# Opening a fused attention and MLP kernel with blocks of 256 keys instead of two blocks of 128

## The chip, the cores and the metric

The kernel runs on one core of a Trainium2 chip. The metric is the device time of one execution in microseconds (us). Before the change three runs gave 542.96, 543.40 and 543.49 us, with a median of 543.4 us.

## The reference

Three layers follow each other on a batch of 2 sequences with 768 tokens and a model width of 512.

- **Attention.** 8 heads of 64. A query sees the first 8 keys of its sequence and the 96 keys up to itself. A linear bias by distance (ALiBi) is added per head, then softmax, then the product with the values.
- **Channel MLP.** `xn = (x - mean) / sqrt(var + 1e-6) * g_ln`, then `x + relu(xn @ w_ch1) @ w_ch2`, with a hidden width of 2048.
- **Token mix.** `theta = x @ w_theta`, `zr = x * cos(theta)`, `zi = x * sin(theta)`, `u = x + w_tok_r @ zr + w_tok_i @ zi` over the tokens, and at last `u + relu(u @ w_ch)`.

Everything is wanted at float32 accuracy. The weights of the MLP and the mix come as 64-bit floats; they are decoded on the chip, and each weight is split into a high and a low part, so that a product becomes three fast matmuls.

## The kernel before, in words

**Tiles.** The 1536 tokens are 12 blocks of 128 (batch 0 has blocks 0 to 5, batch 1 has 6 to 11). The first block of each sequence (0 and 6) has no older keys: its window is its own 128 keys. The other ten have a window of 256: 96 previous keys, 32 global ones, and their own 128. The text calls them 128-key and 256-key blocks. `CHUNKS` (line 28) pairs the blocks and so sets the order `SEQ` in which the attention takes them. Before, it is `[0, 6], [1, 2], [3, 4], [5, 7], [8, 9], [10, 11]`: both 128-key blocks first.

**One block's attention** (lines 181 to 301) goes through the engines in turn. `load_qk` and `load_v` issue its DMAs on SyncE's queue. `scores` does the q-k matmuls on TensorE, two pairs of heads into the PSUM tag "s" and two into "h". `soften` subtracts the maximum on VectorE (line 213, one instruction per head) and takes the exponential on ScalarE (line 220, one per head). `flip_probs` transposes the probabilities on TensorE; ScalarE copies the even pairs out of PSUM (line 261) and VectorE the odd ones (line 263), each tag with one buffer. `values` multiplies with v, `lift_x` copies the sum out (line 286), `finish_x` transposes it and divides by the softmax sum, `layer_norm` normalises, and `make_xt` transposes the result for the MLP.

**The order in time.** Two 128-key blocks run first, pair of heads by pair of heads, in `head_step` (lines 829 to 862). Then comes a loop of cycles (lines 898 to 951) in which TensorE's order is written out by hand, while a planner orders the instructions of the other engines. Cycle t does the scores of the t-th 256-key block, the values of the block before it, and two items of the MLP:

```python
items = [(c, f) for c in range(NCH) for f in GROUPS[0]]
for t in range((LEAD + len(items)) // 2 + 1):
    j = 2 * t - LEAD
```

An item is one chunk of 256 tokens by one of the first four slices of the hidden width: `up` (`mlp_h`, line 421) and `down` (`mlp_o`, line 446). With `LEAD = 2` the items begin in cycle 1, so cycle 0 is attention without MLP beside it. The remaining slices (lines 953 to 977) and the token mix (lines 993 to 1015) come behind the loop.

**Weights.** The MLP needs its first eight weight pieces while the loop runs. `split_w` makes one piece: two decoding instructions on ScalarE (lines 357 and 361), two on VectorE (362 and 363), a rounding on ScalarE (384) and a subtraction on GpSimd (385). `pieces(t)` sets how many have been made by the end of a cycle: two in the head, five by the end of cycle 0, eight by the end of cycle 1.

**Spins.** `spin` (line 75) issues matmuls of zeros whose result nobody reads. They stand in the head and in cycle 0 only: 28 in the head's code and 24 in cycle 0 (tile names spin and idle).

**Bias.** `make_bias` (line 141) makes the bias tables, first the 128-wide ones on VectorE and then the 256-wide ones on ScalarE (line 170). It needs `n_local`, which a small DMA brings (tile words, line 815).

Of the kernel before, what the change touches and what calls it, by code (L numbers as in the profile page):

```python
# [27 lines left out]
CHUNKS = [[0, 6], [1, 2], [3, 4], [5, 7], [8, 9], [10, 11]]  # L28
# [5 lines left out]
PAD = 24  # L34


@with_exitstack
def kernel(ctx, tc, q, kwin, v, n_pair, g_ln, wall, out):
# [10 lines left out]
    SEQ = [t for ts in CHUNKS for t in ts]  # L49
    NCH = len(CHUNKS)  # L50
# [33 lines left out]
    x2 = [x2all[:, t, :] for t in range(NTT)]  # L84
    nhalf = keep.tile([P, 1], F32, name="nhalf")
# [43 lines left out]
    def behind_exp(n):  # L129
        es = ExitStack()  # L130
        es.enter_context(tc.issue_after(maxima[n]))
        es.enter_context(tc.issue_after(exps[n]))
        return es
# [7 lines left out]
    def make_bias():  # L141

        n = WIN + P
        rel, key, a = (at.tile([P, n], F32, tag="xn", name=f"bias_{x}", bufs=3) for x in ("rel", "key", "a"))
        io = dict(allow_small_or_imprecise_dtypes=True)
        v_ = nc.vector
        own = rel[:, P:n].rearrange("p (t c) -> p t c", c=P)
        old, first = slice(0, WIN), slice(WIN, n)
        nc.gpsimd.iota(own, [[0, 2], [-1, P]], base=0, channel_multiplier=1, **io)
        nc.gpsimd.iota(key[:, first], [[1, P]], base=0, channel_multiplier=0, **io)  # L150
        nc.gpsimd.iota(rel[:, 0:PREV], [[-1, PREV]], base=PREV, channel_multiplier=1, **io)
        nc.gpsimd.iota(key[:, PREV:P], [[1, GLOB]], base=0, channel_multiplier=0, **io)
        v_.memset(rel[:, PREV:P], FAR)
        v_.memset(key[:, 0:PREV], FAR)
        v_.memset(key[:, P:WIN], FAR)
        v_.tensor_scalar(a[:, P:n], rel[:, P:n], 0.0, FAR, ALU.is_lt, ALU.mult)
        v_.tensor_tensor(rel[:, P:n], rel[:, P:n], a[:, P:n], ALU.max)
        yield
        load_n()
        for part in (first, old):  # L160
            r, k_, a_ = rel[:, part], key[:, part], a[:, part]
            with behind_maximum(3 if part is old else None):
                v_.tensor_scalar(a_, r, nl, NEG, ALU.is_ge, ALU.mult)
                v_.tensor_scalar(k_, k_, ng, NEG, ALU.is_ge, ALU.mult)
            v_.tensor_tensor(r, a_, r, ALU.subtract)
            v_.scalar_tensor_tensor(r, k_, nl, r, ALU.subtract, ALU.max)
            for h in range(H):
                slope = 2.0 ** (-8.0 * (h + 1) / H)
                if part is old:
                    nc.scalar.activation(bias[h][:, part], r, AF.Copy, scale=slope / SCALE)  # L170
                else:
                    v_.tensor_scalar(bias[h][:, part], r, slope / SCALE, None, ALU.mult)
            yield
# [50 lines left out]
    def scores(b, i, ps_, startup):  # L224
# [9 lines left out]
        s = [ps("h" if (ps_[0] % 2 if startup else ps_[0]) else "s", [P, n, nk], f"s{b}_{i}_{ps_[0]}_{j}") for j in range(2)]  # L234
# [5 lines left out]
        if startup:  # L240
            spin("o", f"spin{b}_{ps_[0]}", 2)
        if startup:
            soften_all(b, i, ps_, s)
# [7 lines left out]
    def flip_probs(b, i, p, startup):  # L251
        nb = 2 if i else 1
        e = e_t.pop((b, i, p))
        pt_tag = ("o" if startup else "m") if p % 2 else "pt"
# [35 lines left out]
    def finish_x(b, i, startup):  # L290
# [5 lines left out]
        xp = ps("o" if startup else "s", [P, H, D], f"xp{t}")  # L296
# [284 lines left out]
    def early_steps():  # L581
# [11 lines left out]
        for t in range(NZ):  # L593
# [16 lines left out]
    def tok_part(b, s, d, part):  # L610

        w, z = toks[b, s], z_t[b * NQ + s]
# [63 lines left out]
    def general():  # L676
# [102 lines left out]
        for b in range(B):  # L779
# [6 lines left out]
            for i in range(NQ):  # L786
                t = b * NQ + i
                ap = ps("o", [P, DM], f"g_a{t}")
                for s in range(NQ):
                    for n in range(2):  # L790
                        at_ = (n * 2 * SA if i * P < SA else n * SB) + i * P
                        wt = w[TOK + s * NT + at_ // DM][:, at_ % DM:at_ % DM + P]
# [21 lines left out]
    words = keep.tile([P, 2, 2], I32, name="words")  # L814
    nc.sync.dma_start(words.rearrange("p n w -> p (n w)"), n_pair.bitcast(I32).partition_broadcast(P))
# [3 lines left out]
    bias_steps = make_bias()  # L819
# [3 lines left out]
    HEAD = len(CHUNKS[0])  # L823
    ROWS = range(NPAIR)

    def behind(n):
        return divmod(n, NPAIR)

    def head_step(n):

        t, p = divmod(n, NPAIR)
        if t < HEAD:
            if p == 0:
                loads_to(t + 2)
            scores(*blocks[t], [p], True)
        for lag, fn in ((2, lambda b, i, p: flip_probs(b, i, p, True)), (3, values)):
            if 0 <= n - lag < HEAD * NPAIR:
                t, p = divmod(n - lag, NPAIR)
                fn(*blocks[t], p)
                if lag == 3 and p == NPAIR - 1:  # L840
                    lift_x(*blocks[t])
                    finish_x(*blocks[t], True)

    spin("m", "spin", 12)
    for n in range(2):
        head_step(n)
    next(bias_steps)
    load_to(1)
    nc.sync.dma_start(gbc, g_ln.partition_broadcast(P))
    for n in range(2, 4):  # L850
        head_step(n)
    for n in range(4, HEAD * NPAIR):
        head_step(n)
        for d, m in enumerate((13, 15)):
            if n == m // 2:
                with behind_exp(m):
                    split_w(0, (d,))
        if n == 7:
            layer_norm(SEQ[0])
    with behind_maximum(7):  # L860
        test_n()

    NB = NTT - HEAD
    LEAD = 2
# [13 lines left out]
    def flips(t, ps_):  # L878
        if 0 <= t < NB:
            for p in ps_:  # L880
                flip_probs(*blocks[HEAD + t], p, False)

    made = []

    def pieces(t):
        n = (3,6)[t] if t < len((3,6)) else 2 * GROUP - 2
        if len(made) < n:
            with behind_exp(len(maxima) - 1):
                while len(made) < n:
                    m = len(made)  # L890
                    split_w(1 + m // 2, (m % 2,))
                    made.append(m)
        elif t >= 4:
            with behind_exp(len(maxima) - 1):
                decode_to(2 * GROUP + min(NW, t - 3))

    last1 = blocks[HEAD - 1]
    with tc.manual_schedule(engines={mybir.EngineType.PE}):
        for t in range((LEAD + len(items)) // 2 + 1):
            j = 2 * t - LEAD  # L900
            if t == 0:
                flip_probs(*last1, 2, True)
                values(*last1, 1)
                flip_probs(*last1, 3, True)
                spin("o", "idle0", 5)
            if t < NB:
                loads_to(HEAD + t + 2)
                sc = [scores(*blocks[HEAD + t], [0, 1], False)]
            if t == 0:
                values(*last1, 2)  # L910
                values(*last1, 3)
                lifted = lift_x(*last1)
            if t < NB:
                sc.append(scores(*blocks[HEAD + t], [2, 3], False))
                soften_all(*blocks[HEAD + t], [0, 1], sc[0])
            if 0 <= t - 1 < NB:
                for p in ROWS:
                    values(*blocks[HEAD + t - 1], p)
                lifted = lift_x(*blocks[HEAD + t - 1])
            if t < NB:  # L920
                with tc.issue_after(lifted):
                    soften_all(*blocks[HEAD + t], [2, 3], sc[1])
            if t == 0:
                spin("o", "idle3", 8)
                make_xt(SEQ[0])
                finish_x(*last1, True)
                layer_norm(SEQ[1])
                flips(0, (0, 1))
                spin("o", "idle1", 8)
                flips(0, (2, 3))  # L930
                make_xt(SEQ[1])
                spin("o", "idle2", 3)
                pieces(0)
                continue
            if t > NB:
                down(j - 1)
            up(j, "s")
            if t <= NB:
                finish_x(*blocks[HEAD + t - 1], False)
                layer_norm(SEQ[HEAD + t - 1])  # L940
            flips(t, (0, 1))
            if t <= NB:
                down(j - 1)
            up(j + 1, "h")
            flips(t, (2, 3))
            if t < NB:
                make_xt(SEQ[HEAD + t - 1])
            down(j)
            if t == NB:
                make_xt(SEQ[HEAD + t - 1])  # L950
            pieces(t)
# [31 lines left out]
    def more(t):  # L983
        if NZ <= t < NTT:
            for _ in theta(t):
# [8 lines left out]
    for n in range(NTT):  # L994
# [4 lines left out]
        for t in (NZ, NZ + 1) if n == 0 else (n + NZ + 1,):  # L999
            if t < NTT:  # L1000
                flip_x(t)
# [69 lines left out]
```

## Time and profile before

| | |
|---|---|
| median of three runs | 543.4 us |
| the profiled execution: its own time | 544.21 us |
| its span, first to last instruction | 542.1 us |
| TensorE matmul (PE) busy | 531.7 us, 98% |
| VectorE (DVE) busy | 361.7 us, 67% |
| ScalarE (ACT) busy | 284.5 us, 52% |
| GpSimd (POOL) busy | 20.3 us, 4% |
| DMA, mean over the span | 91 GB/s |

2.1 us of the profiled execution lie outside its span. A busy TensorE includes the spins, and matmuls overlap in the pipeline, so their pace is read from the distance between starts. PE, PEld, DVE, ACT and POOL are TensorE's matmuls, its weight loads, VectorE, ScalarE and GpSimd; SPq is SyncE's queue. L213 is line 213 of the kernel.

### The profile page before, as it was taken

What the parts mean: (1) busy time and instruction counts of PE and PEld (TensorE: products, weight loads), DVE (VectorE), ACT (ScalarE), POOL (GpSimd) and SP (SyncE); (2) the same over time, 40 slices, a digit from 0 to 9 for tenths busy, and PEclk for the clock granted to TensorE, in tenths of its full rate; (3) what the DMA queues carried; (4) which work ended last, traced back from release to release, by engine and by line L of the source; (5) the groups of instructions that cost most, each with busy time, mean ns of one, the idle gap of its engine ahead of it and who ended that gap; (6) DMA issues with size and microseconds to landing.
All of it is one profiled execution on the core that took longest, in us unless ns stands there. A gap on an engine that the chain in (4) does not pass through costs nothing.

```text
span 542.1 us, 8276 instructions
## 1 busy us (share of the span) xinstructions
PE 531.7 (98%) x3124; PEld 443.7 (82%) x3124; DVE 361.7 (67%) x791; ACT 284.5 (52%) x627; POOL 20.3 (4%) x31
## 2 busy tenths in 40 slices
PE   9998999999999999999999999999999999999996
PEld 4467888888888888888888887888888888888885
DVE  5789777877775455453558777986896689821532
ACT  4789766666734232333237556954885666720200
POOL 1223100100000000000000000000000000000000
PEclk9999999999999999999999999999999999999999
DMA  8946634422030232103224363220300000000122
GB/s 259 310 163 226 232 112 137 137 79 62 18 118 1 79 115 79 39 1 116 79 83 151 110 201 117 79 87 31 119 37 0 1 1 2 1 0 21 58 80 82
DMA packets 18543, 49.11 MB, mean 91 GB/s; under 512 B 2240, under 2 KB 4288, under 8 KB 18496
## 3 DMA queue, kind: packets, MB, share of 16 engines
q1 hardware_dynamic: 18496, 48.51, 26.4%
q8 instruction: 26, 0.43, 0.3%
q14 instruction: 21, 0.17, 0.1%
HBM read 45.35 MB, written 3.15 MB: 89 GB/s over the span
## 4 chain that ended last, share of the span: by engine, by line
PE 91%; ACT 4%; DVE 3%; issue 1%; ACTq 0%
PE op L446 24%; PE hp L421 24%; PE acc L621 18%; PE thm L544 6%; PE ch L667 6%; PE s L239 3%; PE xa L277 3%; PE pt L258 3%; ACT e L220 2%; PE spin L79 1%; PE xp L327 1%; PE xp L298 1%; PE xnp L327 1%; DVE w L363 1%; ACT dec L361 0%
## 5 line engine op out<-in xcount | busy, mean ns | idle before, releaser
L621 PE MATMUL acc<-tokh,z 128*128 128x256 f32 (+1 forms) x384 | 95.4, 336 | 0.0
L421 PE MATMUL hp<-xth,w1h 128*128 128x512 f32 (+1 forms) x240 | 84.3, 351 | 0.3 <-DVE nm L213 0.3
L421 PE MATMUL hp<-xtl,w1h 128*128 128x512 f32 (+1 forms) x240 | 83.2, 347 | 0.0
L421 PE MATMUL hp<-xth,w1l 128*128 128x512 f32 (+1 forms) x240 | 83.1, 346 | 0.0
L426 ACT ACTIVATE hh<-hp 128x512 fp32r<-128x512 f32 (+1 forms) x60 | 30.6, 510 | 97.7 <-PE hp L421 97.5
L446 PE MATMUL op<-w2h,hh 128*128 128x512 f32 x192 | 76.7, 400 | 0.0
L446 PE MATMUL op<-w2h,hl 128*128 128x512 f32 x192 | 75.2, 392 | 0.0
L446 PE MATMUL op<-w2l,hh 128*128 128x512 f32 x192 | 75.0, 390 | 0.0
L621 PEld LDWEIGHTS acc<-tokh,z 128*128 128x128 f32 x384 | 66.5, 190 | 8.0
L426 DVE SCALAR_TENSOR_TENSOR hl<-hp,hh 128x512 fp32r<-128x512 f32 (+1 forms) x60 | 34.8, 581 | 52.0 <-ACT hh L426 51.8
L621 PE MATMUL acc<-tokl,z 128*128 128x512 f32 (+1 forms) x192 | 64.5, 336 | 0.0
L220 ACT ACTIVATE e<-e,nm 128x256 f32<-128x256 f32 (+1 forms) x96 | 46.0, 483 | 23.6 <-DVE nm L213 23.4
L421 PEld LDWEIGHTS hp<-xth,w1h 128*128 128x128 f32 x240 | 45.3, 189 | 8.2 <-ACT e L220 1.2
L421 PEld LDWEIGHTS hp<-xtl,w1h 128*128 128x128 f32 x240 | 45.3, 189 | 6.2 <-DVE xtl L329 0.2
L421 PEld LDWEIGHTS hp<-xth,w1l 128*128 128x128 f32 x240 | 45.3, 189 | 5.6
L361 ACT ACTIVATE dec<-raw 128x512 int32<-128x512 uint32 x58 | 38.5, 664 | 9.6 <-DVE wt L363 5.9
L446 PEld LDWEIGHTS op<-w2h,hl 128*128 128x128 f32 x192 | 36.1, 188 | 8.3 <-DVE hl L426 0.8
L446 PEld LDWEIGHTS op<-w2l,hh 128*128 128x128 f32 x192 | 36.2, 188 | 6.8
L446 PEld LDWEIGHTS op<-w2h,hh 128*128 128x128 f32 x192 | 36.1, 188 | 6.5
L621 PEld LDWEIGHTS acc<-tokl,z 128*128 128x128 f32 x192 | 36.4, 190 | 4.0
L213 DVE CUSTOM_DVE_ANT_0 e<-s,bias 128x256 f32<-128x256 f32 (+1 forms) x96 | 32.8, 396 | 8.7 <-PE s L239 8.5
L520 ACT ACTIVATE tokh<-wt 128x512 fp32r<-128x512 f32 x36 | 22.1, 626 | 23.2 <-PE acc L621 18.1
(131 smaller groups left out, 918.7 us busy)
## 6 DMA issues: line engine op xcount, KB each, us to landing
raw<-in_wall SPq DMA_DIRECT2D x58, 512.0 KB, 3.5
k<-in_kwin SPq DMA_DIRECT2D x10, 512.0 KB, 4.9
q<-in_q SPq DMA_DIRECT2D x12, 256.0 KB, 3.8
vc<-in_v SPq DMA_DIRECT2D x12, 256.0 KB, 4.0
out<-o SPq DMA_DIRECT2D x8, 256.0 KB, 2.0
vw<-in_v SPq DMA_DIRECT2D x10, 192.0 KB, 4.2
out<-o SPq DMA_DIRECT2D x8, 128.0 KB, 2.1
vw<-in_v SPq DMA_DIRECT2D x10, 64.0 KB, 4.0
```

Of the source, the lines that this page charges most:

```text
L213: r = nc.vector.tensor_tensor_reduce(out=e[:, j, :], in0=s[j], in1=bias[h][:, b0:b0 + nk], scale=-SCALE, scalar=3.0e38, op0=ALU.add, op1=A ...
L220: r = nc.scalar.activation(e[:, j, :], e[:, j, :], AF.Exp, bias=nm[:, h:h + 1], scale=-1.0, accum_out=sm[:, h:h + 1])
L239: nc.tensor.matmul(s[j][:, a, :], qb[rows, p, :], kb[rows, p, k0:WIN], start=True, stop=True)
L258: nc.tensor.transpose(pt[:, j, c, :], e[:, j, c * P:(c + 1) * P], ident)
L361: nc.scalar.activation(t, r.bitcast(U32)[:, :, 0], AF.Copy, scale=2.0**-29 * (1 - 2.0**-15), bias=-0.4999)
L421: nc.tensor.matmul(hp, l, r[:, kk, :], start=(n == 0), stop=(n == 3 * KD - 1))
L426: r = nc.scalar.activation(hh, hp, AF.Relu), nc.vector.scalar_tensor_tensor(hl, hp, 0.0, hh.bitcast(F32), ALU.max, ALU.subtract)
L446: nc.tensor.matmul(op_t[c][j], l, r, start=(f == fs[0] and n == 0), stop=(f == fs[-1] and n == 2))
L520: nc.scalar.activation(hi, src, AF.Copy)
L544: nc.tensor.matmul(mp, l[:, kk, :], r[:, kk, :], start=(n == 0), stop=(n == 3 * KD - 1))
L621: mm = nc.tensor.matmul(o, l[:, dsl], r[:, sl], start=first and not (paired and d % 2), stop=end and not (paired and d % 2 == 0))
L667: nc.tensor.matmul(mp, l[:, kk, es], r, start=(kk == 0 and m == 0), stop=(kk == KD - 1 and m == 2))
```

## The change

The head is gone. The order of the blocks becomes `[1, 2], [3, 4], [5, 7], [8, 0], [9, 10], [11, 6]`, so that a 256-key block opens, and the 128-key blocks are the eighth and the last. All twelve go through the loop. `LEAD` becomes 6: the first MLP item stands in cycle 3, and cycles 0, 1 and 2 are attention alone. The scores of the second block are pulled into cycle 0 (`EARLY`). Five pieces of weights are due by the end of cycle 2 and eight by the end of cycle 3. The spins are 11 at the start and 4, 2 and 2 in cycle 0. The bias for 256 keys is made first, two heads on VectorE and six on ScalarE; the bias for 128 keys is made in cycle 5. The first block's q and k come in halves, its k on ScalarE's DMA queue. The test of `n` moves to cycle 8, and the decoding of the second group of weights starts one cycle later relative to the MLP items. The token mix takes its blocks in the order 1, 2, 3, 4, 5, 0 of each sequence, and the host rolls its weights to match. The core of the diff:

```diff
-CHUNKS = [[0, 6], [1, 2], [3, 4], [5, 7], [8, 9], [10, 11]]
+CHUNKS = [[1, 2], [3, 4], [5, 7], [8, 0], [9, 10], [11, 6]]
+DVE_BIAS = 2
+FIRST = 5
+EARLY = 1
+NPIECES = [(0, 1), (1, 3), (3, 5), (5, 8), (8, 8)]
+SPIN0 = 11
+SPINS = [(4, 2, 2)]
...
+    SORD = [*range(1, NQ), 0]
+    TORD = [b * NQ + s for b in range(B) for s in SORD]
...
+        for h in range(H):
+            slope = 2.0 ** (-8.0 * (h + 1) / H)
+            o = bias[h][:, 0:WIN] if old else bias[h][:, WIN:]
+            if h < DVE_BIAS:
+                v_.tensor_scalar(o, rel, slope / SCALE, None, ALU.mult)
+            else:
+                nc.scalar.activation(o, rel, AF.Copy, scale=slope / SCALE)
...
-        nc.sync.dma_start(qb, q[b, i])
-        nc.sync.dma_start(kb[:, :, k0:], kwin[b, i, :, :, k0:])
+        first = not qt
+        for a in ((0, 2), (2, 4)) if first else ((0, 4),):
+            a = slice(*a)
+            nc.sync.dma_start(qb[:, a], q[b, i, :, a])
+            (nc.scalar if first else nc.sync).dma_start(kb[:, a, k0:], kwin[b, i, :, a, k0:])
...
-    for n in range(4, HEAD * NPAIR):
-        head_step(n)
...
-    NB = NTT - HEAD
-    LEAD = 2
+    NB = NTT
+    LEAD = 6
...
     with tc.manual_schedule(engines={mybir.EngineType.PE}):
+        spin("m", "spin", SPIN0)
         for t in range((LEAD + len(items)) // 2 + 1):
             j = 2 * t - LEAD
+            sp = SPINS[t] if t < len(SPINS) else (0, 0, 0)
+            want = NPIECES[min(t, len(NPIECES) - 1)]
+            loads_to(t + 2)
+            score(t, LO)
+            score(t, HI)
+            soften_(t, LO)
             if 0 <= t - 1 < NB:
                 for p in ROWS:
-                    values(*blocks[HEAD + t - 1], p)
+                    values(*blocks[t - 1], p)
...
+            pieces(want[0])
...
+            if sp[0]:
+                spin("o", f"idle{t}", sp[0])
             up(j, "s")
...
+            flips(t, LO)
+            if t < EARLY:
+                score(t + 1, LO)
+                soften_(t + 1, LO)
...
+            if sp[1]:
+                spin("o", f"idle{t}b", sp[1])
             up(j + 1, "h")
+            flips(t, HI)
+            if t < EARLY:
+                score(t + 1, HI)
+            if 0 < t < NB:
+                make_xt(SEQ[t - 1])
+            if sp[2]:
+                spin("o", f"idle{t}c", sp[2])
             down(j)
...
+            if t == FIRST:
+                with behind_exp(len(maxima) - 1):
+                    for _ in make_bias(False):
+                        pass
```

## Rows read from the trace of the kernel before

**Rows 1.** Windows: length, then each engine's busy time (instructions), granted clock, DMA share, GB/s

```profile
7.00:22.95 15.95, 14.67 (x97) 7.64 (x93) 10.37 (x55) 13.38 (x50) 0.52 (x1) 1.00 1.01 355
22.95:34.81 11.86, 10.86 (x73) 6.49 (x72) 10.18 (x33) 9.06 (x26) 3.89 (x4) 1.00 0.56 189
34.81:47.94 13.13, 11.93 (x104) 10.03 (x103) 12.51 (x35) 11.51 (x32) 4.43 (x4) 1.00 0.65 220
47.94:61.40 13.46, 12.51 (x110) 10.87 (x109) 12.79 (x35) 10.31 (x28) 4.40 (x4) 1.00 0.63 217
61.40:135.11 73.71, 73.71 (x649) 65.08 (x648) 56.04 (x185) 47.63 (x142) 4.43 (x6) 1.00 0.33 110
538.00:542.00 4.00, 0.00 (x0) 0.00 (x0) 0.00 (x0) 0.00 (x0) 0.00 (x0) 0.71 0.13 45
```

**Rows 2.** Timeline of TensorE in cycle 3: start, us, line, output and inputs, count

```profile
61.40 2.00 PE L239 MATMUL s<-k,q 64*128 64x256 f32 x16
63.32 0.44 PE L277 MATMUL xa<-pts,vw 128*64 128x128 f32 x4
...
65.22 0.39 PE L421 MATMUL hp<-xth,w1h 128*128 128x256 f32 x1
...
66.75 0.60 PE L298 MATMUL xp<-ident,xs 128*128 128x128 f32 x4
67.19 1.04 PE L258 MATMUL pt<-ident,e 128*128 128x128 f32 x8
67.98 0.48 PE L446 MATMUL op<-w2h,hh 128*128 128x512 f32 x1
...
70.89 1.03 PE L258 MATMUL pt<-ident,e 128*128 128x128 f32 x8
71.76 0.60 PE L327 MATMUL xnp<-ident,xn 128*128 128x128 f32 x4
```

**Rows 3.** Timeline of TensorE in the head, a 128-key block

```profile
14.44 0.72 PE L239 MATMUL s<-k,q 64*128 64x128 f32 x8
15.08 0.44 PE L258 MATMUL pt<-ident,e 128*128 128x128 f32 x2
```

**Rows 4.** Timeline of the start: the spins, the wait for n, the bias of 256 keys

```profile
1.20 5.30 PE L79 MATMUL spin<-zero 128*128 128x512 bf16 x12 [1.20 <-DVE zero L121]
3.55 0.17 DVE L93 CAST low<-words 128x2 f32<-128x2 uint32 x1 [2.13 <-DMA words<-in_n]
11.66 2.55 ACT L170 ACTIVATE bias<-bias_rel 128x256 bf16<-128x256 f32 x8
```

**Rows 5.** Timeline of ScalarE in cycle 0, first and last of eight exponentials, a copy, a decode

```profile
26.76 0.50 ACT L220 ACTIVATE e<-e,nm 128x256 f32<-128x256 f32 x1
...
30.21 0.50 ACT L220 ACTIVATE e<-e,nm 128x256 f32<-128x256 f32 x1
...
31.18 0.59 ACT L261 ACTIVATE pts<-pt 128x512 f32<-128x512 f32 x1
31.66 0.69 ACT L357 ACTIVATE w<-raw 128x512 f32<-128x512 f32 x1
```

**Rows 6.** Timeline of VectorE in cycles 0 and 1: first and last of eight maxima, a copy, a decode

```profile
25.64 0.41 DVE L213 CUSTOM_DVE_ANT_0 e<-s,bias 128x256 f32<-128x256 f32 x1
...
28.04 0.41 DVE L213 CUSTOM_DVE_ANT_0 e<-s,bias 128x256 f32<-128x256 f32 x1
...
34.10 0.68 DVE L263 COPY pts<-pt 128x512 f32<-128x512 f32 x1
...
36.65 1.30 DVE L362 SCALAR_TENSOR_TENSOR dec<-w,dec 128x512 int32<-128x512 int32 x1 [0.25 <-ACT dec L361]
```

**Rows 7.** Timeline of TensorE at the end of cycle 0: spins, then the next cycle's scores

```profile
29.64 1.89 PE L79 MATMUL idle<-zero 128*128 128x512 bf16 x8
...
34.81 2.36 PE L239 MATMUL s<-k,q 64*128 64x256 f32 x16
```

**Rows 8.** SyncE's own waits up to 62 us: who waited for whom, us in total, times, longest

```profile
SPq L345 <- DVE w L363: 26.7, 8, 7.9
```

More of the change, by code (lines that the diff above doesn't have):

```diff
@@ L84 @@
     x2 = [x2all[:, t, :] for t in range(NTT)]
+    words = keep.tile([P, 2, 2], I32, name="words")
+    nc.sync.dma_start(words.rearrange("p n w -> p (n w)"), n_pair.bitcast(I32).partition_broadcast(P))
     nhalf = keep.tile([P, 1], F32, name="nhalf")
@@ L139, in behind_relu, with make_bias @@
         return es
-    def make_bias():
-        n = WIN + P
-        rel, key, a = (at.tile([P, n], F32, tag="xn", name=f"bias_{x}", bufs=3) for x in ("rel", "key", "a"))
+    def make_bias(old):
+        n = WIN if old else P
+        t = [at.tile([P, DM], F32, tag="xn", name=f"bias{old}_{x}", bufs=3) for x in ((0, 1, 2) if old else (0,))]
+        rel, key, a = (x[:, 0:n] for x in t) if old else (t[0][:, x * P:(x + 1) * P] for x in range(3))
+        own = slice(n - P, n)
         io = dict(allow_small_or_imprecise_dtypes=True)
@@ L146, in make_bias @@
         v_ = nc.vector
[L147 to L157, printed above, removed]
-        yield
[L159 to L173, printed above, removed]
+        if old:
+            nc.gpsimd.iota(rel[:, 0:PREV], [[-1, PREV]], base=PREV, channel_multiplier=1, **io)
+            nc.gpsimd.iota(key[:, PREV:P], [[1, GLOB]], base=0, channel_multiplier=0, **io)
+            v_.memset(rel[:, PREV:P], FAR)
+            v_.memset(key[:, 0:PREV], FAR)
+            v_.memset(key[:, P:WIN], FAR)
+        else:
+            nc.gpsimd.iota(key, [[1, P]], base=0, channel_multiplier=0, **io)
@@ new lines, in make_bias @@
+        nc.gpsimd.iota(rel[:, own], [[-1, P]], base=0, channel_multiplier=1, **io)
+        v_.tensor_scalar(a[:, own], rel[:, own], 0.0, FAR, ALU.is_lt, ALU.mult)
+        v_.tensor_tensor(rel[:, own], rel[:, own], a[:, own], ALU.max)
+        yield
+        if old:
+            load_n()
+        v_.tensor_scalar(a, rel, nl, NEG, ALU.is_ge, ALU.mult)
+        v_.tensor_scalar(key, key, ng, NEG, ALU.is_ge, ALU.mult)
+        v_.tensor_tensor(rel, a, rel, ALU.subtract)
+        v_.scalar_tensor_tensor(rel, key, nl, rel, ALU.subtract, ALU.max)
@@ L222, in soften, with scores @@
         e_t[b, i, p] = e
-    def scores(b, i, ps_, startup):
+    def scores(b, i, ps_):
         nk = WIN if i else P
@@ L233, in scores @@
         n = len(ps_)
-        s = [ps("h" if (ps_[0] % 2 if startup else ps_[0]) else "s", [P, n, nk], f"s{b}_{i}_{ps_[0]}_{j}") for j in range(2)]
+        s = [ps("h" if ps_[0] else "s", [P, n, nk], f"s{b}_{i}_{ps_[0]}_{j}") for j in range(2)]
         k0 = WIN - nk
@@ L295, in finish_x @@
         nc.vector.reciprocal(sm, sm)
-        xp = ps("o" if startup else "s", [P, H, D], f"xp{t}")
+        xp = ps("s", [P, H, D], f"xp{t}")
         for p in range(NPAIR):
@@ L591, in fill @@
                 next(ahead)
-        for t in range(NZ):
+        for t in TORD[:NZ]:
             while t not in ready:
@@ L822 @@
     loads_to(1)
-    HEAD = len(CHUNKS[0])
+    load_to(0)
     ROWS = range(NPAIR)
[L826 to L845, printed above, removed]
-        head_step(n)
[L847 to L851, printed above, removed]
-    for n in range(4, HEAD * NPAIR):
[L853 to L861, printed above, removed]
-    NB = NTT - HEAD
-    LEAD = 2
+    NB = NTT
+    LEAD = 6
     items = [(c, f) for c in range(NCH) for f in GROUPS[0]]
@@ L880, in flips, with pieces @@
             for p in ps_:
-                flip_probs(*blocks[HEAD + t], p, False)
+                flip_probs(*blocks[t], p)
     made = []
-    def pieces(t):
-        n = (3,6)[t] if t < len((3,6)) else 2 * GROUP - 2
+    def pieces(n):
         if len(made) < n:
@@ L890, in pieces, with score, soften_ @@
                     m = len(made)
-                    split_w(1 + m // 2, (m % 2,))
+                    split_w(m // 2, (m % 2,))
                     made.append(m)
[L893 to L897, printed above, removed]
+    sc = {}
+    def score(t, ps_):
+        if t < NB and (t, ps_) not in sc:
+            sc[t, ps_] = scores(*blocks[t], ps_)
+    def soften_(t, ps_):
+        if (t, ps_) in sc and sc[t, ps_]:
+            soften_all(*blocks[t], ps_, sc[t, ps_])
+            sc[t, ps_] = None
@@ L898 @@
+    LO, HI = (0, 1), (2, 3)
     with tc.manual_schedule(engines={mybir.EngineType.PE}):
+        spin("m", "spin", SPIN0)
         for t in range((LEAD + len(items)) // 2 + 1):
             j = 2 * t - LEAD
[L901 to L908, printed above, removed]
@@ L935 @@
+                lifted = lift_x(*blocks[t - 1])
+            with tc.issue_after(lifted) if t else ExitStack():
+                soften_(t, HI)
+            if t == 0:
+                nc.sync.dma_start(gbc, g_ln.partition_broadcast(P))
+            pieces(want[0])
             if t > NB:
                 down(j - 1)
+            if sp[0]:
+                spin("o", f"idle{t}", sp[0])
             up(j, "s")
-            if t <= NB:
-                finish_x(*blocks[HEAD + t - 1], False)
-                layer_norm(SEQ[HEAD + t - 1])
@@ L941 @@
-            flips(t, (0, 1))
+            if 0 < t <= NB:
+                finish_x(*blocks[t - 1])
+                layer_norm(SEQ[t - 1])
+            flips(t, LO)
+            if t < EARLY:
+                score(t + 1, LO)
+                soften_(t + 1, LO)
             if t <= NB:
                 down(j - 1)
+            if sp[1]:
+                spin("o", f"idle{t}b", sp[1])
             up(j + 1, "h")
-            flips(t, (2, 3))
-            if t < NB:
-                make_xt(SEQ[HEAD + t - 1])
+            flips(t, HI)
@@ L948 @@
+            if t < EARLY:
[4 more added lines that the diff above has]
+                spin("o", f"idle{t}c", sp[2])
             down(j)
             if t == NB:
-                make_xt(SEQ[HEAD + t - 1])
-            pieces(t)
+                make_xt(SEQ[t - 1])
+            pieces(want[1])
+            if want[1] == 2 * GROUP and t >= 7:
+                with behind_exp(len(maxima) - 1):
+                    decode_to(2 * GROUP + min(NW, t - 6))
@@ L953 @@
+            if t == FIRST:
+                with behind_exp(len(maxima) - 1):
+                    for _ in make_bias(False):
+                        pass
+            if t == 8:
+                with behind_exp(len(maxima) - 1):
+                    test_n()
     work = [(g, c, f) for g in range(1, len(GROUPS)) for c in range(len(WIDE)) for f in GROUPS[g]]
@@ L981, with more @@
     p2b_es, p2["b"] = stack(name="p2b", bufs=1)
-    def more(t):
-        if NZ <= t < NTT:
-            for _ in theta(t):
+    def more(n):
+        if NZ <= n < NTT:
+            for _ in theta(TORD[n]):
                 pass
```

48 lines of the change are left out of this document (12 added, 36 removed).

## The prediction

> **What bounds the kernel now.** I read the page first: TensorE is busy 98% of the span, so only TensorE time that is empty, or filled with spins, can be won. Then the busy time by windows, cut where each cycle's scores begin [rows 1]. From 61.40 to 135.11 us TensorE is busy 73.71 of 73.71 us: six cycles of 12.29 us bound by it, with VectorE and ScalarE at about three quarters and two thirds. Up to 61.40 us it is another kernel. In the two cycles before (13.13 and 13.46 us) VectorE works 12.51 and 12.79 us; in cycle 0 (11.86 us) it works 10.18 us, and there TensorE's busy time holds spins, such as the eight in 1.89 us [rows 7]. So all that the change can move lies before the point where TensorE gets its first closed cycle. I call that point S5 for the new kernel (the scores of cycle 5), which answers to 61.40 us (the scores of cycle 3) in the old one, as both have done four ups and three downs there.
>
> **What is left behind that point.** The old kernel has finished two 128-key blocks and is inside its third 256-key block; the new one is inside its fifth 256-key block and still owes both 128-key ones. All the rest is the same work, so the new kernel has less left, by two differences between a 256-key and a 128-key block. By starts in cycle 3 [rows 2], a 256-key block costs 63.32 - 61.40 = 1.92 us of scores, 65.22 - 63.32 = 1.90 us of values, and 0.79 + 0.87 = 1.66 us of flips (67.19 to 67.98, 70.89 to 71.76). A 128-key block has the same number of score instructions at half the columns: eight of its sixteen take 15.08 - 14.44 = 0.64 us [rows 3], so 1.28 us, not half. It has half the flips and half the values matmuls. The difference is 0.64 + 0.83 + 0.95 = 2.42 us, twice that 4.84 us. This holds if cycles 7, 8, 11 and 12 stay bound by TensorE. VectorE and ScalarE get less to do in them than in the six full cycles, where they have 56.0 and 47.6 of 73.7 us [rows 1], so I take all of it. If nothing of it came, the term would be 0.
>
> The sum is then: change = (S5 - 61.40) - 4.84.
>
> **The start.** Eleven spins instead of twelve at 5.30 / 12 = 0.44 us put the first scores at 1.20 + 4.86 = 6.06 us [rows 4]. They need half a q and half a k, less than the whole ones that the old kernel has by its first scores. The two k issues on ScalarE cost at most 1.3 us there (0.65 us for the old k issue) and lie before its first need. The bias cannot start before words lands (3.55 us); four 256-wide VectorE steps and the casting are about 1.7 us (estimate, from the 2.17 us that the old tables took from the same instant), so it is ready at 5.2 us. Six of the eight tables on ScalarE at 2.55 / 8 = 0.32 us [rows 4] end at 7.1 us, one instruction after VectorE has its first maxima.
>
> **Cycles 0 to 2.** The exponentials run at (30.21 - 26.76) / 7 = 0.49 us each, a copy or decode step at 31.66 - 31.18 = 0.48 to 0.56 us [rows 5], the maxima at (28.04 - 25.64) / 7 = 0.34 us [rows 6]. Along the chain:
> - Cycle 0: eight exponentials, 7.1 to 11.0. Copy, second flips, the pulled scores, four spins, values: 0.5 + 0.9 + 1.0 + 1.0 + 1.9, with about 0.2 for waits: 16.5 with the lift.
> - Cycle 1: the second block's first four exponentials are done in cycle 0; the last four with a maximum ahead: 2.4, to 18.9. Copy, flips, transposition for the MLP (0.4, estimate from the xp row): 2.2 with a wait, to 21.1.
> - Cycle 2: scores. In the old kernel they took 2.36 instead of 1.92 us behind such a transposition [rows 7], so 23.5. Values 25.4; lift, four exponentials and half a microsecond of weights on ScalarE, 28.7; copy, flips, transposition, 31.0.
>
> VectorE gives the other bound. From the pulled maxima (done at about 12.5 us) to that point it has: maxima of two blocks less the four already done, 12 x 0.34 = 4.1; five copies at 0.6, 3.0; two normalisations with the division, 2 x 2.25 = 4.5 (sum of five instructions by their spacing, estimate); two subtractions for the MLP, 1.2; three weight pieces at 1.2, and 0.6 for one of their steps that runs at 1.30 instead of about 0.68 us beside GpSimd [rows 6], 4.2. That is 17.0 us, and at the share that it reaches in the old cycles 1 and 2 (0.95) 17.9: 30.4. With the pulled maxima ending later, as they share VectorE with copies, I take S3 = 32.0 for the first scores of cycle 3. The old kernel stands at the same point, with five pieces due and two not finished, at 34.81 us. From there cycles 3 and 4 have the instructions of the old cycles 1 and 2, so S5 = 32.0 + 13.13 + 13.46 = 58.6.
>
> **Other edits.** The bias of 128 keys in cycle 5: three GpSimd instructions, some 1.5 us each on VectorE and ScalarE, beside 12.29 us of TensorE with over 2.9 us free on both: 0, and at most 1.5 us if it stood in the chain. Later decoding: the last pieces still come before the second group's first product; 0, at most 0.6 us a piece. The test of n: 0. The new mixing order leaves the count of matmuls; none of my rows shows a wait that it takes away or adds: 0, between -0.5 and +0.5.
>
> **Sum.** 58.6 - 61.4 - 4.84 = -7.6 us. The profiled execution took 544.2 us (542.1 of span and 2.1 around it): 536.6 for it. It lies 0.8 us above the median, so 535.8 us against 543.4. The ends: if VectorE never holds cycles 3 and 4, S5 is about 32.0 + 11 + 12.3 = 55.3, 532.5 us; if S3 is 3 us later, 538.8 us.
>
> **The clock.** The granted clock is 1.00 in every window up to 135 us, and 0.71 in the last four, where TensorE has no instruction left [rows 1]. The start shows what the low level costs: spins at 0.44 us there, and at 1.89 / 8 = 0.24 later [rows 4, 7]. The new cycles 1 and 2 have no spin and gaps of up to 1.5 us; the old kernel shows no such stretch without spins. [...]
>
> **Rivals.**
> [...]
> 2. The other side: VectorE and the chain through it keep the old pace. Each opening cycle takes 11.86 us, as the one old cycle without MLP does [rows 1]. S3 is 6.06 + 3 x 11.86 = 41.6, S5 68.2, +2.0: 545.4 us. It decides where S3 passes 34.81 + 4.84 = 39.65, that is above 11.2 us a cycle. Against it: that old cycle also finishes a 128-key block, normalises and transposes twice, and holds 19 spins.
> [...]
> 4. Transfers. The old start loads at 355 GB/s with the queue full to 22.95 us [rows 1]. Four whole blocks, g_ln and five pieces are 8.0 MB, 22.5 us of it, so from 2 us to about 25: enough, unless SyncE stops behind raw buffers, where it waited 26.7 us in all [rows 8]. Three microseconds lost: 538.8.
> 5. The cycles with 128 keys stay at 12.29 us, held by something else than TensorE: -2.8, 540.6 us.
>
> **How the numbers follow.** Forecast 0.61, with its own range from 532 to 540. Rival 1 once 0.10, twice 0.07; rival 2 0.07; rival 3 0.04; rival 4 0.06; rival 5 0.05. Runs of this kernel can tell about 0.2% (1.1 us) from no change. Faster: 0.61 + 0.10 + 0.06 + 0.05 = 0.82. Same: rival 1 twice, 0.07. Slower: rivals 2 and 3, 0.11. From 532 to 542 us holds the forecast, rival 1 once, and rivals 4 and 5: 0.82.
>
> **What would show it.** First scores at 6 us, S3 near 32 and S5 near 58.6, full cycles of 12.29 us after, and cycles 7 to 8 and 11 to 12 shorter by 2.4 us for each block. [...] The prediction is wrong if S3 comes after 36 us, or if something behind the loop moves by more than 0.5 us.

## The result, and the profile after

The changed kernel takes 537.6 us (median of five runs, 537.46 to 538.23) against 543.4 us (five runs, 542.96 to 543.92). The ratio is 0.9895, with a 95% interval of 0.9881 to 0.9910. The gain of 5.8 us lies inside the predicted range; the forecast was 7.6 us. The profiled execution took 537.60 us with a span of 535.8 us, 6.6 us less than the profiled one before, which lay 0.8 us above its median. The span is 6.3 us shorter.

The windows of the changed kernel, cut at its own cycles, have the columns of [rows 1]: length, busy time of PE, PEld, DVE, ACT and POOL, granted clock, DMA share, GB/s.

```profile
8.36:23.07 14.71, 11.64 (x95) 7.64 (x94) 11.19 (x41) 13.57 (x44) 1.84 (x2) 1.00 1.04 381
23.07:33.87 10.80, 7.79 (x73) 6.03 (x72) 10.11 (x31) 9.58 (x27) 3.04 (x3) 1.00 0.91 306
33.87:46.88 13.01, 12.14 (x104) 9.98 (x103) 11.51 (x34) 11.39 (x31) 3.55 (x4) 1.00 0.57 185
46.88:60.23 13.35, 12.51 (x110) 10.87 (x109) 12.79 (x35) 9.87 (x27) 4.79 (x6) 1.00 0.63 198
60.23:84.80 24.57, 24.57 (x217) 21.69 (x217) 18.48 (x67) 15.02 (x50) 1.10 (x2) 1.00 0.32 109
84.80:95.38 10.58, 10.58 (x102) 9.50 (x101) 7.17 (x30) 6.69 (x24) 0.55 (x1) 1.00 0.38 125
95.38:106.80 11.42, 11.42 (x93) 9.98 (x93) 10.65 (x42) 7.97 (x24) 0.92 (x1) 1.00 0.38 121
106.80:131.37 24.57, 24.57 (x217) 21.70 (x216) 19.29 (x63) 16.15 (x48) 1.47 (x2) 1.00 0.18 60
```

The reader is to see three stages. From the first exponential (8.36 us) to cycle 3 (33.87) ScalarE works 23.15 of 25.51 us, VectorE most of the second half, and TensorE has gaps. Cycles 3 and 4 (13.01 and 13.35 us) are those that were cycles 1 and 2 before, with nearly the same busy times [rows 1]. From 60.23 us on TensorE is closed. Full cycles still take 12.29 us; cycle 7, with the first 128-key block's scores and flips, takes 10.58, and cycle 8, with its values, 11.42.

The closed stretch that began at 61.40 us now begins at 60.23: 1.17 us. The first 128-key block gives 2 x 12.29 - 10.58 - 11.42 = 2.58 us. The second is read from TensorE's timelines: the scores of the last block and the first of its values, first in the changed kernel, then in the one before.

```profile
131.37 1.16 PE L255 MATMUL s<-k,q 64*128 64x128 f32 x16
141.95 1.09 PE L289 MATMUL xa<-pts,vc 128*64 128x128 f32 x16
...
135.11 2.00 PE L239 MATMUL s<-k,q 64*128 64x256 f32 x16
147.40 0.44 PE L277 MATMUL xa<-pts,vw 128*64 128x128 f32 x4
```

From one to the other it takes 10.58 us in place of 12.29, and the values themselves 1.02 us (the next product starts at 142.97) in place of 1.90 [rows 2]: 1.71 + 0.88 = 2.59 us. So the two 128-key blocks give 5.17 us where they stand, and the prediction had 4.84.

How much of it arrives is read where the token mix begins. The first token-mix product and the last, in one row for its line (duration, first and last start), after and before:

```profile
L633 PE MATMUL acc<-tokh,z x384: 277/336/478, 372.6 to 508.5; 128*128 128x512 f32 x96, 128*128 128x256 f32 x96
...
L621 PE MATMUL acc<-tokh,z x384: 277/336/476, 378.6 to 514.6; 128*128 128x512 f32 x96, 128*128 128x256 f32 x96
```

That is 6.0 us earlier at the first and 6.1 at the last, so the token mix keeps its length. 1.17 + 5.17 = 6.34 us were won up to the last values, so some 0.3 us are lost again between them and the token mix; what loses them is not shown.

The first instructions of the chain, from VectorE's and ScalarE's timelines of the changed kernel (the line numbers are its own):

```profile
3.75 0.17 DVE L103 CAST low<-words 128x2 f32<-128x2 uint32 x1 [2.33 <-DMA words<-in_n]
3.96 0.16 DVE L104 SCALAR_TENSOR_TENSOR nval<-words,low 128x2 f32<-128x2 int32 x1
4.23 0.35 DVE L176 TENSOR_SCALAR biasTrue<-biasTrue,nval 128x256 f32<-128x256 f32 x1
4.50 0.22 DVE L170 TENSOR_SCALAR biasTrue<-biasTrue 128x128 f32<-128x128 f32 x1
4.75 0.29 DVE L171 TENSOR_TENSOR biasTrue<-biasTrue,biasTrue 128x128 f32<-128x128 f32 x1
...
6.51 1.95 ACT L185 ACTIVATE bias<-biasTrue 128x256 bf16<-128x256 f32 x6 [3.35 <-DVE biasTrue L178]
8.36 0.49 ACT L236 ACTIVATE e<-e,nm 128x256 f32<-128x256 f32 x1
```

The bias was forecast for 5.2 us and ScalarE's tables for 7.1; they came at 6.5 and 8.4. L170 and L171 do not need n, and yet they stand behind the two instructions that wait for it. TensorE's waits in cycles 0 to 2 are on the copies and the lift of ScalarE, 5.2 us in all, but for 0.48 us on VectorE. Those of cycle 1:

```profile
18.22 0.66 PE L310 MATMUL xp<-ident,xs 128*128 128x128 f32 x4 [0.70 <-ACT xs L298]
18.71 1.04 PE L270 MATMUL pt<-ident,e 128*128 128x128 f32 x8
21.45 1.25 PE L270 MATMUL pt<-ident,e 128*128 128x128 f32 x8 [1.71 <-ACT pts L273]
22.54 0.60 PE L339 MATMUL xnp<-ident,xn 128*128 128x128 f32 x4
```

The granted clock stays at 1.00 in every window above, though from 17.5 to 23.1 us TensorE has transposes alone, with gaps of up to 1.71 us and no spin.

### The profile page after: what moved, and what is told of

Read it like the earlier page. It is cut to its first block, busy times and chain, and to the rows that moved or that the text cites. A ratio compares the mean times of both kernels' runs of the same rounds, so it can differ in the third digit from the quotient of the medians.

```text
span 535.8 us, 8220 instructions
## 1 busy us (share of the span) xinstructions
PE 522.2 (97%) x3091; PEld 439.7 (82%) x3091; DVE 361.0 (67%) x789; ACT 284.3 (53%) x631; POOL 19.6 (4%) x32
## 4 chain that ended last, share of the span: by engine, by line
PE 90%; ACT 5%; DVE 3%; issue 1%; DMA 1%; ACTq 0%; DVEq 0%
PE op L458 24%; PE hp L433 24%; PE acc L633 19%; PE thm L556 6%; PE ch L679 6%; PE pt L270 3%; PE xa L289 3%; PE s L255 2%; ACT e L236 2%; PE xp L339 1%; PE xp L310 1%; PE xnp L339 1%; DVE w L375 1%; DMA words<-in_n 1%; DVE e L229 1%
## 5 line engine op out<-in xcount | busy, mean ns | idle before, releaser
L446 DVE SCALAR_TENSOR_TENSOR x2all<-op,rsall,x2all 128x512 f32<-128x512 f32 x48 | 33.3, 741 | 2.1 <-PE op L458 2.1
```

The lines of the kernel that those rows point to most:

```text
L446: nc.vector.scalar_tensor_tensor(x2[t], o, rsall[:, t:t + 1], x2[t], ALU.mult, ALU.add)
```

## The experiments

All times are medians of four runs beside the kernel before on the same chip, which took 543.25 to 543.57 us there; the changed kernel's is 537.6 us. "Cycle 3" and "cycle 5" are the starts of their scores, 33.87 and 60.23 us in the changed kernel.

**1. The bias chain.** The mis-sized term: does the late bias hold the opening?

```diff
-        v_.tensor_tensor(rel[:, own], rel[:, own], a[:, own], ALU.max)
+        last = v_.tensor_tensor(rel[:, own], rel[:, own], a[:, own], ALU.max)
         yield
         if old:
-            load_n()
+            with tc.issue_after(last.ins):
+                load_n()
```

> The two VectorE steps on the causal half of the 256-key bias (0.58 us from 4.50 to 5.08) are done before n arrives instead of after it. If the table chain holds the first exponentials, as I read the trace of the changed kernel, they begin at about 7.9 instead of 8.36 us, every later point of the opening moves by as much, and the time falls by 0.4 to 0.5 us to about 537.1. If something later in cycles 0 to 2 (VectorE, the weight pieces) is the true bound, the first exponentials come earlier but cycle 3 still begins at 33.9 us: 537.6.

Measured: 536.87 us, ratio to before 0.9879 (0.9863 to 0.9896). Both steps now run ahead of n, and the tables begin 0.73 us earlier:

```profile
1.82 0.23 DVE L170 TENSOR_SCALAR biasTrue<-biasTrue 128x128 f32<-128x128 f32 x1 [0.39 <-POOL biasTrue L169]
2.08 0.29 DVE L171 TENSOR_TENSOR biasTrue<-biasTrue,biasTrue 128x128 f32<-128x128 f32 x1
...
5.78 1.95 ACT L186 ACTIVATE bias<-biasTrue 128x256 bf16<-128x256 f32 x6 [2.62 <-DVE biasTrue L179]
7.90 0.51 ACT L237 ACTIVATE e<-e,nm 128x256 f32<-128x256 f32 x1 [0.17 <-DVE nm L230]
```

The first exponential comes 0.46 us earlier, cycle 3 at 33.42 (0.45 earlier) and cycle 5 at 59.79 (0.44). The start is on the chain, one for one. The exponential now waits 0.17 us for a maximum, and VectorE for scores from TensorE, so the other 0.27 us of the tables' gain are lost to the next wait. The profiled run is the slowest of the four (537.71 us): its token mix still begins 0.6 us earlier (372.0 us), and what it loses stands behind the last token-mix product.

**2. The order of the blocks alone.** The new loop, without a head, takes the blocks in the old order.

```diff
-CHUNKS = [[1, 2], [3, 4], [5, 7], [8, 0], [9, 10], [11, 6]]
+CHUNKS = [[0, 6], [1, 2], [3, 4], [5, 7], [8, 9], [10, 11]]
...
-FIRST = 5
+FIRST = 0
...
-    SORD = [*range(1, NQ), 0]
+    SORD = [*range(NQ)]
...
-    bias_steps = make_bias(True)
+    bias_steps = make_bias(False)
...
-                    for _ in make_bias(False):
+                    for _ in make_bias(True):
```

> The new loop without a head, but with the blocks and the token mix in the old order: both 128-key blocks open the loop, the 128-key bias is made first and the 256-key bias at the end of cycle 0. My theory: the opening is bound by ScalarE and VectorE, to which a 128-key block is only some 1.3 us cheaper, while the later cycles lose the 5.16 us of TensorE that the 128-key blocks give there; with 1.3 us more of tables in the opening, cycle 3 begins at about 32 to 33 us and the time is 540 to 541.5. If the order were the whole gain: 543.4. If dropping the head were the whole gain (the opening as much shorter as the later cycles get longer): 537.6.

Measured: 540.69 us, ratio to before 0.9948 (0.9928 to 0.9968): between the two kernels, as my theory had it. So neither the order nor the loop is the whole gain. Cycle 3 begins at 31.42 (32 to 33 was expected), only 2.45 us earlier than in the changed kernel; the token mix begins at 375.2, 2.6 us later, so the old order loses some 5 us behind the opening. But the split is not clean. The windows of this kernel show another thing:

```profile
6.00:16.71 10.71, 8.35 (x73) 5.45 (x72) 8.46 (x52) 10.60 (x44) 0.43 (x1) 1.00 1.02 370
16.71:23.53 6.82, 5.01 (x21) 4.21 (x23) 6.17 (x17) 5.79 (x17) 2.19 (x3) 0.50 1.05 367
23.53:31.42 7.89, 4.91 (x46) 3.65 (x43) 7.19 (x23) 7.16 (x23) 2.26 (x3) 1.00 0.80 280
```

The granted clock was 0.50 from 16.71 to 23.53 us, and TensorE's timeline there has a wait of 3.07 us, from 15.45 to 18.52, and then slow scores. The clock fell 1.3 us into that wait.

```profile
18.52 1.12 PE L270 MATMUL pt<-ident,e 128*128 128x128 f32 x4 [3.07 <-ACT pts L273]
19.43 1.06 PE L339 MATMUL xnp<-ident,xn 128*128 128x128 f32 x4
20.42 3.79 PE L255 MATMUL s<-k,q 64*128 64x256 f32 x16
```

Scores cost 3.71 us there (20.42 to 24.13) instead of 1.92. All four runs show a mean clock below the changed kernel's (0.997 to 0.999): 540.02 and 540.24 us at 0.996, 541.13 at 0.993, 541.54 at 0.990. A straight line through these four points gives about 539.4 us at 0.999 (an estimate). So of the 3.1 us that the old order costs, some 1.2 would be the clock. How much the order is worth at a steady clock stays open.

**3. The order of the token mix.** The changed kernel with the old one.

```diff
-    SORD = [*range(1, NQ), 0]
+    SORD = [*range(NQ)]
...
-    tok = np.roll(tok.reshape(S // P, P, -1, DM), -1, axis=0).transpose(0, 2, 1, 3).reshape(-1, P, DM)
+    tok = tok.reshape(S // P, P, -1, DM).transpose(0, 2, 1, 3).reshape(-1, P, DM)
```

> The changed kernel with the token mix in the old order 0 to 5, and the host's weights unrolled. By the prediction's row for this edit the time is the same, 537.6 within 0.5. The rival: block 0 now gets its MLP result only in the second of three wide chunks, so the four early theta products cannot start before it; they are squeezed behind the last group's second chunk, and TensorE waits at the start of the token mix: 1 to 3 us more, 538.6 to 540.6.

Measured: 537.59 us. The edit is worth nothing measurable, and the rival falls: the first token-mix product starts at 372.4 us, against 372.6.

**4. The spins of cycle 0.**

```diff
-SPINS = [(4, 2, 2)]
+SPINS = []
```

> The changed kernel without the eight spins of cycle 0 (those at the very start stay). My theory: they stand where TensorE waits for ScalarE anyway, so that their removal changes nothing: 537.6 within 0.4, granted clock 1.00 in cycles 0 to 2. [...] A third possibility: the spins themselves delay the pulled scores, and the time falls by up to 1 us.

Measured: 537.63 us. TensorE's waits up to 62 us grow from 8.7 to 10.5 us in all, and cycle 5 begins at 60.12. In the profiled run the clock stays at 1.00; the three other runs show a mean of 0.995 or 0.996, at 537.51 to 537.66 us, below all five of the changed kernel. A fall like the one in experiment 5 below, 3.41 us at 0.50, takes 0.003 off the mean (an estimate: half of 3.41 over 536 us). So the clock most likely gives way in some runs without them. These runs left no trace, so where it fell is not shown; their times show no loss.

**5. Two pieces of weights later.**

```diff
-NPIECES = [(0, 1), (1, 3), (3, 5), (5, 8), (8, 8)]
+NPIECES = [(0, 0), (0, 1), (1, 3), (3, 8), (8, 8)]
```

> The changed kernel with two weight pieces fewer before cycle 3 (0, 1 and 3 at the ends of cycles 0 to 2 instead of 1, 3 and 5) and five instead of three in cycle 3. My theory: ScalarE and VectorE bound the stretch up to the first closed cycle as a sum, so the place of a piece hardly counts: cycle 3 begins up to 3 us earlier (near 31), cycle 5 within 1 us of 60.2, the time 537.6 within 1. The rival: in cycles 0 to 2 the pieces fill time in which both engines wait, so cycle 3 begins at 33.5 as before and cycles 3 and 4 get longer by two pieces: 540 to 541.

Measured: 540.51 us. My theory falls. Cycle 3 begins at 32.04, 1.83 us earlier, so two pieces cost 0.9 us each in cycles 0 to 2; but cycle 5 begins at 63.31. The waits of TensorE from 40 to 64 us (who waits for whom, us in total, times, longest), and a window with the columns of [rows 1]:

```profile
PE hp L433 <- ACT w1h L396: 1.8, 2, 1.4
PE hp L433 <- POOL w1l L397: 1.7, 2, 0.9
...
52.63:56.04 3.41, 3.41 (x18) 3.41 (x17) 1.91 (x4) 3.32 (x11) 1.28 (x1) 0.50 0.85 281
```

The up-projections wait 3.5 us for their weights: a piece goes through ScalarE, VectorE, ScalarE and GpSimd, and five of them in one cycle come too late. Part of the loss is the clock: behind these waits it fell to 0.50 for 3.41 us in which TensorE was busy throughout, about 1.7 us of lost work (an estimate, half of the window). The run with the highest mean clock (0.998) took 539.62 us, still 2.0 us above the changed kernel. The rival had the time right, but not that cycle 3 would begin as before. When a piece is due counts, and not only the sum of the work.

**6. ScalarE or VectorE.**

```diff
-        if p % 2 == 0:
+        if p == 0 or p == 2 and SEQ.index(b * NQ + i) > 2:
             nc.scalar.activation(pts, pt, AF.Copy)
```

> In the first three blocks the copy of the third pair's flips goes from ScalarE to VectorE: ScalarE loses 3 x 0.48 us, VectorE gains 3 x 0.60. If ScalarE bounds cycles 0 to 2 (my reading: the exponentials carry the chain from 8.4 to 12.4, 18.9 to 20.9 and 29.5 to 31.5), cycle 3 begins about 1 us earlier and the time is 536.6. If VectorE does, cycle 3 begins 1 to 1.8 us later: 538.6 to 539.4.

Measured: 537.89 us, cycle 3 at 34.34 and cycle 5 at 60.26. Neither forecast: with 1.4 us less on ScalarE and 1.8 us more on VectorE (the sizes expected) cycle 3 came 0.47 us later, where 1 us earlier or 1 to 1.8 us later was forecast. I read from it that neither engine alone bounds the opening.

**7. More scores pulled forward.**

```diff
-EARLY = 1
+EARLY = 3
```

> The scores of blocks 2 and 3 are pulled into cycles 1 and 2 as those of block 1 are pulled into cycle 0. If ScalarE's waits at each cycle's begin cost time (it idles 1.1 of 14.7 us before cycle 2 and 1.2 of 10.8 us in it), the time falls by 0.6 to 1.5 us, to 536.1 to 537.0. The rival: the pulled exponentials stand in ScalarE's queue ahead of the lift and the copies that TensorE waits for, and the time is 0.5 to 2 us longer: 538.1 to 539.6.

Measured: 538.45 us, the rival's time but not its cause. TensorE waits 3.3 us for VectorE before the transpositions for the MLP, where the rival had the lift and the copies late, and cycle 5 begins at 61.27. This trace too has a fall of the clock, with TensorE busy throughout:

```profile
38.00:41.42 3.42, 3.42 (x28) 3.09 (x25) 2.84 (x6) 2.56 (x7) 1.27 (x1) 0.50 0.51 167
```

The run with the highest mean clock (0.998) took 538.18 us, no more than the slowest run of the changed kernel (538.23). So pulling three shows no gain, and what it would cost at a steady clock stays open.

**8. What the low words of the weights cost.** In `decode` the first eight pieces return after the high words, so that one instruction on ScalarE and two on VectorE are left out for each piece. The weights then lack their low words.

```diff
         nc.scalar.activation(out, r.bitcast(F32)[:, :, 1], AF.Copy, scale=2.0**-112)
+        if 0 <= n < 2 * GROUP and i == n and at_open[0]:
+            return
...
```

> The first eight weight pieces are decoded without their low words (one ScalarE and two VectorE instructions left out for each, so the weights are wrong). It measures what the weights cost the opening now. If they are what keeps VectorE and ScalarE behind, cycle 3 begins near 30, cycles 3 and 4 fall to TensorE's own time (about 10.9 and 12.3 us), cycle 5 begins at 53 to 54 and the time is about 531. If the chain of one block through TensorE, VectorE and ScalarE sets the opening, cycle 3 begins at 33, cycle 5 at 56 to 57, and the time is 534 to 535.

Measured: 534.04 us, ratio 0.9830 (0.9814 to 0.9847): the chain's forecast. Its windows:

```profile
8.38:22.46 14.08, 11.62 (x95) 7.57 (x93) 9.43 (x39) 12.82 (x42) 1.69 (x2) 1.00 1.04 371
22.46:32.41 9.95, 7.80 (x73) 6.04 (x73) 7.02 (x27) 8.70 (x26) 3.14 (x4) 1.00 1.04 348
32.41:44.19 11.78, 11.77 (x104) 9.98 (x103) 8.14 (x30) 10.53 (x30) 4.67 (x6) 1.00 0.82 274
44.19:56.47 12.28, 12.28 (x110) 10.84 (x109) 8.16 (x29) 7.74 (x24) 3.11 (x5) 1.00 0.52 163
```

Cycles 0 to 2 are only 1.46 us shorter, though VectorE is relieved to 7.02 of 9.95 us in cycle 2. I read what is left there as the chain of one block through TensorE, VectorE and ScalarE; ScalarE, at 12.82 of 14.08 and 8.70 of 9.95 us, has the least room in it. Cycles 3 and 4 lose 2.3 us and are closed: there the decoding of the weights is what held TensorE.

**9. No scores pulled forward.**

```diff
-EARLY = 1
+EARLY = 0
```

> The changed kernel without pulling block 1's scores into cycle 0. My theory: ScalarE is left with less to do between 12.4 and 18 us, the lift of block 0 comes 1 us later behind the unpulled scores, and cycle 3 begins 0.5 to 1.5 us later: 538.1 to 539.1. The rival: pulling only changes the order, as it did when it was extended to cycles 1 and 2 (there it cost 0.85 us), and the time is 536.8 to 537.6.

Measured: 538.55 us. Cycle 3 begins 0.91 us later (34.78), as forecast. Pulling one block is worth about a microsecond; experiment 7 shows no more from three.

**10 to 12. Three steps on experiment 1.**

```diff
-DVE_BIAS = 2
+DVE_BIAS = 4
```

> Experiment 1 with four instead of two of the 256-key bias tables on VectorE and so four instead of six on ScalarE. If the tables on ScalarE still hold the first exponential (7.90 us in experiment 1), it comes at 7.6 and the time falls by another 0.3 us to 536.6. The rival: VectorE's maxima are delayed by two tables of 0.25 us, and nothing is won: 536.9 to 537.2.

Measured: 536.95 us, the first exponential at 7.89 as in experiment 1: the rival's time, but not for its reason. The first maxima, at 7.43 us in both, wait for the first scores; in the changed kernel they come at 7.14. So what the tables would be worth behind scores that come as early is not shown.

```diff
-NPIECES = [(0, 1), (1, 3), (3, 5), (5, 8), (8, 8)]
+NPIECES = [(0, 0), (1, 3), (3, 5), (5, 8), (8, 8)]
...
+            if t == 0:
+                with behind_exp(len(maxima) - 1):
+                    decode_to(1)
```

> Experiment 10, and the rounding of the first weight piece goes behind the last four exponentials of block 1 (its decoding stays in cycle 0). In the changed kernel the exponentials wait for it from 18.1 to 18.9 us, on the chain. If the place of a piece inside a cycle counts, cycle 2 begins 0.5 to 0.8 us earlier than in experiment 10 and the time is 535.9 to 536.2. The rival: the engines catch up at cycle 2, where VectorE stands behind, and nothing is won.

Measured: 536.94 us. The last four exponentials of block 1 begin at 17.55 us instead of 18.40 in experiment 10 (0.27 us of it stood there from the first exponential on), but cycle 2 begins at 22.56 against 22.63: the engines catch up there. The rival.

```diff
-            (nc.scalar if first else nc.sync).dma_start(kb[:, a, k0:], kwin[b, i, :, a, k0:])
+            (nc.scalar if first and a.start == 0 else nc.sync).dma_start(kb[:, a, k0:], kwin[b, i, :, a, k0:])
...
-SPIN0 = 11
+SPIN0 = 10
```

> Experiment 11, the second half of block 1's k back on SyncE's queue, and one spin less at the start. In the changed kernel the first half of q lands at 5.70 us, behind both halves of k, against 4.4 us for the whole q in the kernel before. If the first q then lands before 5 us, the first scores begin at 5.6, the first exponential 0.2 to 0.4 us earlier than in experiment 11, and the time falls by as much. The rival: the bias tables hold the maxima anyway, and the time is that of experiment 11.

Measured: 537.35 us, 0.4 above experiment 11, which is less than single times can tell. The first exponential does come at 7.06 us, 0.56 earlier. Then TensorE's timeline shows the pulled scores of the next block waiting for their k:

```profile
6.69 1.13 PE L256 MATMUL s<-k,q 64*128 64x256 f32 x8 [0.39 <-DMA k<-in_kwin]
...
10.95 1.14 PE L256 MATMUL s<-k,q 64*128 64x256 f32 x8 [1.29 <-DMA k<-in_kwin]
```

Cycle 3 begins at 33.62, 0.50 later than in experiment 11. Neither forecast. With an earlier start the transfers become the bound: the DMA share is 1.04 from 8 to 23 us in the changed kernel already. Experiments 1, 10 and 11 end within 0.1 us of each other, 0.7 us below the changed kernel; as single times that is less than the 0.2% that can be told, but each of their traces has cycle 3 and cycle 5 0.4 to 0.8 us earlier.

## Why the prediction was right, step by step

- **Where to look.** Right: nothing behind the loop moved by more than some 0.3 us, and the sum made of S5 and of the late 128-key blocks is the gain: 1.17 + 5.17 = 6.34 of the span's 6.3 us.
- **The late 128-key blocks, 4.84 us.** Right to 0.33. The cycles stayed closed, as [rows 1] gave reason to expect. The scores were cheaper than forecast: 1.10 us for sixteen in a row, where [rows 3] gave 1.28. The 0.3 us lost before the token mix nearly undo the difference, which is luck.
- **First scores at 6.06 us.** 5.98. But the step's reason, that half a q and half a k come sooner than whole ones, was wrong: the first half of q took 4.5 us to land, where the whole q took 3.2 before, with both halves of k ahead of it on the other queue. In experiment 12, with the second half of k behind it on its own queue, it took 3.2 us again. It landed at 5.70, just in time; in experiments 6, 7 and 9 the first scores wait 0.5 to 0.8 us for it.
- **The bias at 5.2 us.** The mis-sized term: the tables were ready at 6.45. Two more steps than I counted, 0.58 us, stand on VectorE between n and the tables, as the planner put the causal half behind the wait. The 2.17 us that the estimate came from hold the same two steps of the old kernel, at 3.83 and 4.23 us, and I left them out. The casts and the four wide steps took 2.12 us where I had 1.7, and n came 0.20 us later than before. Up to rounding these make the 1.25 us, of the 1.87 by which S3 (33.87) missed 32.0. Experiment 1 gains 0.45 us of it at cycle 3.
- **Cycles 0 to 2, the rest of S3.** 8.36 to 33.87 is 25.5 us, where 7.1 to 32.0 was forecast: 24.9. The 32.0 lay 1.0 us above the chain's own 31.0, so the chain was short by 1.6. Two terms that it lacks stand on ScalarE ahead of the last four exponentials of block 1, a lift and the rounding of a weight piece:

```profile
17.56 0.60 ACT L298 ACTIVATE xs<-xa 128x512 f32<-128x512 f32 x1 [0.72 <-PE xa L289]
18.32 0.63 ACT L396 ACTIVATE w1h<-w 128x512 fp32r<-128x512 f32 x1 [0.16 <-DVE w L375]
18.86 0.49 ACT L236 ACTIVATE e<-e,nm 128x256 f32<-128x256 f32 x1
```

The forecast names the lift at 16.5 us but has no term for it, and none for the rounding: its terms up to there are the copy, flips, scores, spins and values. That the margin, taken for VectorE, covered most of it is in part luck. The two bounds, chain and VectorE, were forecast close together, and experiment 6 fits that. Experiment 8 shows that the low words of the weights are 1.5 us of it.
- **Cycles 3 and 4 as the old 1 and 2.** 26.36 us against 26.59.
- **The clock.** It did not fall in this kernel: 1.00 with no spins in cycles 1 and 2 and gaps of up to 1.71 us. The chances of a fall (rival 1 with 0.10 and 0.07, rival 3 with 0.04) were my estimate: no row of the kernel before has a fall while TensorE works, and no run shows why one comes. What the runs show in its place: in experiment 2 the clock was 0.50 from 1.3 us into a wait of 3.07 us on, and scores took 3.71 us there instead of 1.92. It fell to 0.50 in the traces of experiments 5 and 7 too (for 3.41 and 3.42 us), and most likely in three runs of experiment 4. So a fall can come with small edits of the opening, and that none came here is in part luck.
- **The other edits, put at 0.** Experiment 3 priced the mixing order: 0. The bias of 128 keys and the test of n stand in cycles 5 and 8, where TensorE is busy throughout (24.57 of 24.57 and 11.42 of 11.42 us). The later decoding was not run alone.
- **The old pace of 11.86 us a cycle.** The opening took (33.87 - 5.98) / 3 = 9.3 us a cycle: under the 11.2 from which it would have lost.
- **Transfers.** They did not hold the changed kernel: the chain up to cycle 3 has no DMA after n. Experiment 12 shows them next, with the first exponential half a microsecond further on than in experiment 11.

By the sum, -7.6 was forecast and -6.0 arrived at the token mix; the miss is S5, 60.23 instead of 58.6. The profiled gain was 6.6 us and that of the medians 5.8; the difference is where the one profiled execution before lay, as the prediction said.

## What to carry to other kernels

When one engine is closed from some point on, price a reordering by two numbers: when that point comes, and how much of the closed engine's work is still owed there. An order that leaves the cheap blocks for the closed stretch gains their difference there, 5.17 us here, and pays for it in the opening: with the cheap blocks first the closed stretch came 2.46 us earlier, even with a clock that fell (57.77 against 60.23 us, experiment 2). In the opening a chain of several engines need not be one engine's bound: moving 1.4 us from ScalarE to VectorE moved nothing forward, while 0.46 us at the first link came through as 0.45. And weights made beside it must be placed by when they are due, not by the total.

## What the runs showed of the hardware

- A second DMA queue did not bring an urgent load sooner. With k issued ahead of it on ScalarE's queue, q's first half (128 KB) landed 4.5 us after its issue; with the second half of k behind it on SyncE's own queue, after 3.2 us (experiment 12).
- TensorE was slower at the very start, up to about where the trace's record of the granted clock begins, at full speed; ahead of that nothing is recorded. In the changed kernel it begins at 5.89 us: the eleven spins from 1.19 us on took 0.44 us each (4.85 us), the four from 7.91 us on started 0.22 us apart. In the kernel before it begins at 7.23 us: four score products of 128 keys from 6.43 us on took 0.80 us, four from 7.71 us on 0.49. In the changed kernel the first scores (5.98) took 1.93 us, and the first maxima, which waited 0.20 us for them, came at 7.14 us. In experiment 1 they came at 7.43, behind a wait of 1.21 us for the scores.
- In the changed kernel the clock stayed at 1.00 through 5.5 us of transposes with gaps of up to 1.71 us. In experiment 2 it fell to 0.50 1.3 us into a wait of 3.07 us, behind transposes; in experiment 5 it fell to 0.50 0.9 us behind waits of 1.44 and 0.85 us; in experiment 7, where TensorE's longest wait was 2.0 us, it was 0.50 from 38.00 to 41.42 us. So in these traces the length of a gap alone does not say whether it falls.
